# Float64 weights rounded to float32 by integer steps, with four raw blocks in flight and q, k loaded two head pairs ahead, in a routed attention and squared-ReLU kernel

## The chip, the cores and the metric

One core of one Trainium2 chip runs the whole kernel. The metric is the device time of one execution in microseconds (us). The kernel before takes 1234.09 us, the median of 3 runs (1233.55 to 1234.19).

## What is computed

The first part is attention in which a query sees only the keys of its own cluster: q and k rows are assigned to the nearest of 16 centroids per head. The second part is a feed-forward block on the result. Batch 4, 8 heads, 768 positions, head size 64; model size 512, inner size 2048.

```python
q_assign = np.argmax(np.einsum('bhsd,hcd->bhsc', q_n, c_n), axis=-1)   # q_n, c_n: unit length
k_assign = np.argmax(np.einsum('bhsd,hcd->bhsc', k_n, c_n), axis=-1)
scores = np.where(q_assign[..., :, None] == k_assign[..., None, :], scale * q @ k.T, -1e9)
attn = softmax(scores) @ v
x = attn.transpose(0, 2, 1, 3).reshape(B * S, H * D)
r = np.maximum(x @ w_in, 0.0)
return ((r * r) @ w_out).astype(np.float32)
```

q, k, v and the centroids are float32. w_in (512 x 2048) and w_out (2048 x 512) are float64, 16.8 MB together, and the kernel brings them to float32 itself.

## The kernel before

**Attention.** Heads are worked in 16 pairs (4 batches x 4 pairs). For a pair, `prep` turns q and k by matrix products into qkT (`turn`, three parts), makes the products with the centroids (`logits`) and the cluster numbers (`route`), and for the first batch one-hot masks (`turn_onehot`), for the others spread cluster numbers (`spread`). Then each half of the queries goes over 6 chunks of 128 keys: `scores` makes the products sc, ScalarE the exponentials ex (L337), and GpSimd adds them up in acc: five additions (L347, L351) for six exponentials. `times_v` multiplies by v, and `finish` divides by the sums: VectorE makes rb, ok and xT (L376 to L382).

**The unit.** The program is one list of 96 units; a unit is two key chunks of one pair and half, so two exponentials. The first 24 units are the first batch, all first halves before all second halves. `times_v` runs two units late.

**Feed-forward.** `ffn` is cut into steps, one matrix product each, that the main loop strews between the units as fill: ph (L395) with w_in, gT by ScalarE (L402) and squared by VectorE (L403), then po (L408) with w_out, osb and the store. The first fill stands behind unit 14. What fill is left after the last unit runs at the end.

**The weights.** A block is 128 rows of 512 weights; there are 16 of w_in and 16 of w_out. `load_weights` brings one raw block (512 KB, pool wstage, two buffers) as pairs of 32-bit words lo and hi. `round_weights` makes float32 of it: VectorE cuts out the exponent (w_power, L126), ScalarE shifts its origin (L129), VectorE bounds it (L130) and joins the sign (L134), VectorE cuts out the upper fraction (L139), ScalarE brings it and lo to floating point (L142, L143), GpSimd adds the two (L144) and multiplies by the power (L145). The temporary w_power has one buffer. The main loop asks for 4/3 blocks per unit in the first 12 units, then for two.

```python
for _ in range(2):
    load_weights(next(loaded))
...
rounding += 4 / 3 if u < 12 else 2
while rounding >= 1:
    rounding -= 1
    i = next(to_round, None)
    if i is not None:
        round_weights(i)
```

**What sets the order.** A scheduler at build time puts each engine's instructions in one fixed row, from the program's order and its own estimate of times. On the chip each engine takes its row in order. All loads and stores are issued by SyncE (SP), also in a fixed order; a load waits there until its buffer is free, and what is behind it waits too.

**The end.** The sums of `finish` are checked: good is reduced to one number (L512 ff.), a product every (L515) and a comparison make flag, and all engines read flag and jump over a general path that is not taken with these inputs.

Of the kernel before, what the change touches and what calls it, by code (L numbers as in the profile page):

```python
# [17 lines left out]
P = 128  # L18
UP = 2.0 ** 40
BIG = 2.0 ** 80  # L20


@with_exitstack
def kernel(
# [22 lines left out]
    NG = B * HP  # L47
    SCALE = float(D) ** -0.5
# [3 lines left out]
    loads = ctx.enter_context(tc.tile_pool(name="loads", bufs=3))  # L52
# [8 lines left out]
    xtp = ctx.enter_context(tc.tile_pool(name="xtp", bufs=3))  # L61
    gtp = ctx.enter_context(tc.tile_pool(name="gtp", bufs=FT))
    outp = ctx.enter_context(tc.tile_pool(name="outp", bufs=1))
    wstage = ctx.enter_context(tc.tile_pool(name="wstage", bufs=2))
    wtmp = ctx.enter_context(tc.tile_pool(name="wtmp", bufs=1))
# [52 lines left out]
    def round_weights(i):  # L118
        dst = weights[i][0]
        w = raw_w.pop(i)  # L120
        lo, hi = w[:, :, 0], w[:, :, 1]
        lo_f, hi_f = lo.bitcast(F32), hi.bitcast(F32)
        power = wtmp.tile([P, NW], U32, name="w_power")
        power_f = power.bitcast(F32)

        nc.vector.tensor_scalar(  # L126
            out=power, in0=hi, scalar1=0x7FF00000, scalar2=None, op0=ALU.bitwise_and
        )
        nc.scalar.activation(out=power_f, in_=power, func=ACT.Relu, bias=rebias, scale=1.0)  # L129
        nc.vector.tensor_scalar(  # L130
            out=power, in0=power_f, scalar1=float(255 << 20), scalar2=8.0,
            op0=ALU.min, op1=ALU.mult,
        )
        nc.vector.scalar_tensor_tensor(  # L134
            out=power, in0=hi, scalar=0x80000000, in1=power,
            op0=ALU.bitwise_and, op1=ALU.bitwise_or,
        )

        nc.vector.tensor_scalar(  # L139
            out=hi, in0=hi, scalar1=0x000FFFFF, scalar2=None, op0=ALU.bitwise_and  # L140
        )
        nc.scalar.activation(out=hi_f, in_=hi, func=ACT.Copy, bias=1.0, scale=2.0 ** -20)  # L142
        nc.scalar.mul(out=lo_f, in_=lo, mul=2.0 ** -52)  # L143
        nc.gpsimd.tensor_tensor(out=hi_f, in0=hi_f, in1=lo_f, op=ALU.add)  # L144
        nc.gpsimd.tensor_tensor(out=dst, in0=hi_f, in1=power_f, op=ALU.mult)  # L145


    cen = const.tile([P, D], F32, name="cen")
    nc.sync.dma_start(cen, centroids.rearrange("h c d -> (h c) d"))
    load_qk(0)  # L150
    load_v(0)
# [11 lines left out]
    rebias = const.tile([P, 1], F32, name="rebias")  # L163
    nc.vector.memset(rebias, -float((1023 - 127) << 20))
# [545 lines left out]
```

## Time and profile before

| | |
|---|---|
| median of 3 runs | 1234.09 us |
| the profiled execution's own time | 1233.24 us |
| its span in the trace | 1231.4 us |
| TensorE (PE) busy | 1135.8 us, 92% |
| VectorE (DVE) busy | 578.6 us, 47% |
| GpSimd (POOL) busy | 381.3 us, 31% |
| ScalarE (ACT) busy | 336.2 us, 27% |
| granted TensorE clock, mean | 0.953 |

PEld is TensorE's weight load, which runs beside its products. Times of instructions are from the profile of that one execution; "idle before, releaser" tells how long the engine stood before an instruction and what ended that. A float32 product is two instructions in the profile and one in the order rows below.

### The profile page before, as it was taken

How to read it: one execution, taken by the hardware profiler on the slowest of the kernel's cores; microseconds unless marked ns; L12 is line 12 of the kernel's file. 1: busy time of each engine (PE TensorE's matmuls, PEld its weight loads, DVE VectorE, ACT ScalarE, POOL GpSimd, SP SyncE). 2: the span in 40 equal slices, each digit the busy share in tenths (PEclk: the TensorE clock that was granted, in tenths of full speed). 3: DMA queues.
4: the chain of work that ended last, by engine and by line, in shares of the span. 5: the costliest groups of instructions: out<-in, count | busy, mean ns of one | idle time of the engine just before them, and what ended most of it. 6: DMA issues, size and time to landing. Idle time of an engine off the chain costs nothing.

```text
span 1231.4 us, 10628 instructions
## 1 busy us (share of the span) xinstructions
PE 1135.8 (92%) x4115; PEld 516.2 (42%) x4115; DVE 578.6 (47%) x795; ACT 336.2 (27%) x543; POOL 381.3 (31%) x233
## 2 busy tenths in 40 slices
PE   6677776689999999999999999999999999999997
PEld 3223232234444444444444444444444544554553
DVE  4466746441386865566445654266345653210110
ACT  4433343432233323232212231223212221110110
POOL 2655655442143433432232322233132332000000
PEclk7877798879999999999999999999999999999999
DMA  6332222211201101101001010201000000000000
GB/s 177 87 93 75 79 69 82 90 52 38 56 1 38 39 1 48 47 9 39 1 18 48 1 39 9 56 1 26 9 9 22 1 1 18 9 1 18 9 9 20
DMA packets 63881, 44.30 MB, mean 36 GB/s; under 512 B 51536, under 2 KB 56656, under 8 KB 63824
## 3 DMA queue, kind: packets, MB, share of 16 engines
q1 hardware_dynamic: 63824, 43.56, 12.4%
q8 instruction: 34, 0.56, 0.2%
q14 instruction: 23, 0.19, 0.0%
HBM read 37.26 MB, written 6.29 MB: 35 GB/s over the span
## 4 chain that ended last, share of the span: by engine, by line
PE 77%; POOL 8%; issue 8%; DVE 4%; ACT 2%; DMA 0%; SPq 0%; POOLq 0%; ACTq 0%
PE po L408 27%; PE ph L395 24%; PE sc L325 10%; PE av L357 9%; POOL acc L351 3%; POOL w_raw L144 2%; PE sm L372 2%; PE pt L227 2%; POOL w_out L145 1%; POOL w_in L145 1%; DVE w_power L126 1%; PE pb L303 1%; PE lg L243 1%; ACT ex L337 1%; DVE ids L269 0%
## 5 line engine op out<-in xcount | busy, mean ns | idle before, releaser
L395 PE MATMUL ph<-xT,w_in 128*128 128x384 f32 x1024 | 361.6, 502 | 27.4 <-ACT gT L402 26.3
L351 POOL TENSOR_TENSOR acc<-acc,ex 128x768 f32<-128x768 f32 x128 | 245.9, 1921 | 398.1 <-DVE ex L339 322.6
L408 PE MATMUL po<-w_out,gT 128*128 128x512 f32 x768 | 349.9, 602 | 0.0
L339 DVE SCALAR_TENSOR_TENSOR ex<-qid,ids,ex 128x384 f32<-128x384 bf16 x288 | 229.1, 847 | 157.9 <-ACT ex L337 157.7
L395 PEld LDWEIGHTS ph<-xT,w_in 128*128 128x128 f32 x1024 | 189.9, 193 | 186.9 <-issue 32.3
L408 PEld LDWEIGHTS po<-w_out,gT 128*128 128x128 f32 x768 | 140.5, 191 | 175.1 <-issue 170.6
L325 PE MATMUL sc<-qkT 64*128 64x384 f32 x768 | 195.0, 546 | 12.2 <-ACT ex L337 12.2
L337 ACT ACTIVATE ex<-sc 128x768 f32<-128x768 f32 x192 | 148.1, 806 | 197.0 <-PE sc L325 152.3
L403 DVE TENSOR_TENSOR gT<-gT 128x384 f32<-128x384 f32 x128 | 91.8, 721 | 177.7 <-ACT gT L402 177.4
L357 PE MATMUL av<-ex,v_raw 128*64 128x384 f32 x768 | 161.9, 521 | 0.0
L402 ACT ACTIVATE gT<-ph 128x384 f32<-128x384 f32 x128 | 62.5, 488 | 250.8 <-PE ph L395 250.8
L325 PEld LDWEIGHTS sc<-qkT 64*128 64x128 f32 x768 | 77.0, 197 | 105.1 <-issue 64.2
L376 DVE RECIPROCAL rb<-sm 128x384 f32<-128x384 f32 x32 | 81.7, 2554 | 80.6 <-PE sm L372 80.6
L347 POOL TENSOR_TENSOR acc<-ex 128x768 f32<-128x768 f32 x32 | 58.4, 1826 | 174.7 <-DVE ex L339 153.3
L357 PEld LDWEIGHTS av<-ex,v_raw 128*64 128x64 f32 x768 | 50.8, 141 | 93.3 <-issue 91.5
L126 DVE TENSOR_SCALAR w_power<-w_raw 128x512 uint32<-128x512 uint32 x32 | 32.6, 1020 | 78.0 <-POOL w_out L145 39.9
L415 ACT COPY osb<-po 128x512 f32<-128x512 f32 x24 | 14.0, 585 | 176.2 <-PE po L408 145.9
L144 POOL TENSOR_TENSOR w_raw<-w_raw 128x512 f32<-128x512 f32 x32 | 33.3, 1040 | 79.9 <-ACT w_raw L142 79.9
L129 ACT ACTIVATE w_power<-w_power,rebias 128x512 f32<-128x512 uint32 x32 | 23.1, 722 | 82.0 <-DVE w_power L126 82.0
L307 ACT CAST qid<-pb 128x384 bf16<-128x384 f32 x48 | 21.9, 480 | 40.2 <-PE pb L303 40.0
L142 ACT ACTIVATE w_raw<-w_raw 128x512 f32<-128x512 uint32 x32 | 21.4, 668 | 41.7 <-DVE w_raw L139 41.7
L372 PE MATMUL sm<-acc,ups 128*64 128x384 f32 x128 | 30.2, 536 | 2.7 <-ACT gT L402 2.7
(70 smaller groups left out, 423.2 us busy)
## 6 DMA issues: line engine op xcount, KB each, us to landing
w_raw<-in_moe_w_in_dram SPq DMA_DIRECT2D x16, 512.0 KB, 3.8
w_raw<-in_moe_w_out_dram SPq DMA_DIRECT2D x16, 512.0 KB, 3.5
v_raw<-in_v_dram SPq DMA_DIRECT2D x20, 384.0 KB, 3.2
q_raw<-in_q_dram SPq DMA_DIRECT2D x32, 192.0 KB, 3.6
k_raw<-in_k_dram SPq DMA_DIRECT2D x32, 192.0 KB, 3.2
out_dram<-osb SPq DMA_DIRECT2D x24, 256.0 KB, 2.0
cen<-in_centroids_dram SPq DMA_DIRECT2D x1, 32.0 KB, 1.7
```

What stands on the lines that cost most here:

```text
L144: nc.gpsimd.tensor_tensor(out=hi_f, in0=hi_f, in1=lo_f, op=ALU.add)
L325: nc.tensor.matmul(sc[:, e, 0:TB], lhsT=qkT[pair][rows, NCH + c], rhs=qkT[pair][rows, NB * h : NB * (h + 1)], start=True, stop=pair >= HP,)
L337: nc.scalar.activation(out=t, in_=sc[:, :, 0:TB], func=ACT.Exp, scale=SCALE)
L339: nc.vector.scalar_tensor_tensor(out=t[:, e], in0=qid[pair][1][:, h, e], scalar=ids[pair][:, c % NB, 2 + c // NB, e : e + 1], in1=t[:, e], ...
L347: nc.gpsimd.tensor_tensor(out=acc[pair, h], in0=ex[pair, h, 0], in1=t, op=ALU.add)
L351: nc.gpsimd.tensor_tensor(out=acc[pair, h], in0=acc[pair, h], in1=t, op=ALU.add)
L357: nc.tensor.matmul(av[pair, h][D * e : D * (e + 1)], lhsT=raw_v[pair][:, e, c], rhs=ex[pair, h, c][:, e], start=(c == 0), stop=(c == NCH - 1),
L376: nc.vector.reciprocal(out=rb, in_=sm)
L395: nc.tensor.matmul(ph, lhsT=w_in[:, kk, f * P : (f + 1) * P], rhs=xT[b, h][:, kk], start=(kk == 0), stop=(kk == KT - 1),)
L402: nc.scalar.activation(out=gT[f], in_=ph, func=ACT.Relu)
L403: nc.vector.tensor_tensor(out=gT[f], in0=gT[f], in1=gT[f], op=ALU.mult)
L408: nc.tensor.matmul(po, lhsT=gT[f][:, i * P : (i + 1) * P], rhs=w_out[:, f], start=(f == 0), stop=(f == FT - 1),)
```

## The change

`round_weights` becomes six steps. ScalarE takes the absolute value of hi, read as a float32, into the weight's place (L131) and makes of lo a small number beside 2.0 (L133). VectorE bounds the first (L136) and shifts it left by three bits (L140), and joins the sign of hi to the second (L143). GpSimd adds the two as 32-bit integers (L147). There is no temporary any more, and the constant rebias goes.

The raw blocks have four buffers instead of two. q and k are loaded two pairs ahead (pool loads with four buffers instead of three), v up to three units ahead, and the first v behind the first preparation. The loop asks for 3/2 blocks per unit in the first 12 units. To make room, the raw blocks and three start-up tiles lie in a part of the memory that is closed after the last block; the third xT buffer and two osb buffers (before: one) are opened there. best and ok share a buffer. The check of the sums is written ahead of the left-over fill.

```diff
+    AHEAD = 4
-    loads = ctx.enter_context(tc.tile_pool(name="loads", bufs=3))
+    loads = ctx.enter_context(tc.tile_pool(name="loads", bufs=4))
-    xtp = ctx.enter_context(tc.tile_pool(name="xtp", bufs=3))
+    xtp = ctx.enter_context(tc.tile_pool(name="xtp", bufs=2))
-    outp = ctx.enter_context(tc.tile_pool(name="outp", bufs=1))
-    wstage = ctx.enter_context(tc.tile_pool(name="wstage", bufs=2))
-    wtmp = ctx.enter_context(tc.tile_pool(name="wtmp", bufs=1))
+    early = ExitStack()
+    wstage = early.enter_context(tc.tile_pool(name="wstage", bufs=AHEAD, side="right"))
+    once_early = early.enter_context(tc.tile_pool(name="once_early", bufs=1, side="right"))
+    later = {}
...
     def round_weights(i):
-        dst = weights[i][0]
+        dst = weights[i][0].bitcast(U32)
         w = raw_w.pop(i)
         lo, hi = w[:, :, 0], w[:, :, 1]
-        nc.vector.tensor_scalar(
-            out=power, in0=hi, scalar1=0x7FF00000, scalar2=None, op0=ALU.bitwise_and
-        )
-        nc.scalar.activation(out=power_f, in_=power, func=ACT.Relu, bias=rebias, scale=1.0)
+        nc.scalar.activation(out=dst.bitcast(F32), in_=hi.bitcast(F32), func=ACT.Abs)
+        nc.scalar.activation(
+            out=lo.bitcast(F32), in_=lo, func=ACT.Copy, bias=2.0, scale=2.0 ** -51
+        )
         nc.vector.tensor_scalar(
-            out=power, in0=power_f, scalar1=float(255 << 20), scalar2=8.0,
-            op0=ALU.min, op1=ALU.mult,
+            out=dst.bitcast(F32), in0=dst.bitcast(F32), scalar1=2.0 ** -15, scalar2=HIGHEST,
+            op0=ALU.max, op1=ALU.min,
+        )
+        nc.vector.tensor_scalar(
+            out=dst, in0=dst, scalar1=3, scalar2=None, op0=ALU.logical_shift_left
         )
         nc.vector.scalar_tensor_tensor(
-            out=power, in0=hi, scalar=0x80000000, in1=power,
-            op0=ALU.bitwise_and, op1=ALU.bitwise_or,
-        )
-        nc.vector.tensor_scalar(
-            out=hi, in0=hi, scalar1=0x000FFFFF, scalar2=None, op0=ALU.bitwise_and
-        )
-        nc.scalar.activation(out=hi_f, in_=hi, func=ACT.Copy, bias=1.0, scale=2.0 ** -20)
-        nc.scalar.mul(out=lo_f, in_=lo, mul=2.0 ** -52)
-        nc.gpsimd.tensor_tensor(out=hi_f, in0=hi_f, in1=lo_f, op=ALU.add)
-        nc.gpsimd.tensor_tensor(out=dst, in0=hi_f, in1=power_f, op=ALU.mult)
+            out=lo, in0=hi, scalar=0x80000000, in1=lo, op0=ALU.bitwise_and, op1=ALU.bitwise_or
+        )
+        dst, lo = dst.bitcast(I32), lo.bitcast(I32)
+        nc.gpsimd.tensor_tensor(out=dst, in0=dst, in1=lo, op=ALU.add)
...
     load_qk(0)
-    load_v(0)
+    load_qk(1)
...
             raw.pop(pair)
-            load_qk(pair + 1)
+            load_qk(pair + 2)
...
-            xT[b, h] = xtp.tile([P, KT, TB], F32, name="xT")
+            pool = xtp if (2 * b + h) % 3 < 2 else later["xT"]
+            xT[b, h] = pool.tile([P, KT, TB], F32, name="xT")
...
-    for _ in range(2):
+    for _ in range(AHEAD):
         load_weights(next(loaded))
...
-            if c == 0 and pair not in raw_v:
-                load_v(pair)
+            if c == 0 and u + 3 < len(units) and units[u + 3][0] not in raw_v:
+                load_v(units[u + 3][0])
...
-        rounding += 4 / 3 if u < 12 else 2
+        rounding += 3 / 2 if u < 12 else 2
...
+            elif not later:
+                early.close()
+                for name, bufs in (("xT", 1), ("out", 2)):
+                    later[name] = ctx.enter_context(
+                        tc.tile_pool(name=name + "_late", bufs=bufs, side="right",
+                                     reuse_waits="tile")
+                    )
```

How the instructions move is seen on two engines.

GpSimd, the first blocks, before (w_raw with a number is one raw block, w_in the rounded weights, acc the sums of exponentials):

```order
L144 TENSOR_TENSOR w_raw_263<-w_raw_263 128x512
L145 TENSOR_TENSOR w_in_109<-w_raw_263,w_power_367 128x512
L351 TENSOR_TENSOR acc_251<-acc_251,ex_351 128x768
L351 TENSOR_TENSOR acc_251<-acc_251,ex_359 128x768
L144 TENSOR_TENSOR w_raw_316<-w_raw_316 128x512
L145 TENSOR_TENSOR w_in_109<-w_raw_316,w_power_409 128x512
L347 TENSOR_TENSOR acc_403<-ex_394,ex_401 128x768
```

and with the change:

```order
L351 TENSOR_TENSOR acc_258<-acc_258,ex_366 128x768
L147 TENSOR_TENSOR w_in_106<-w_in_106,w_raw_266 128x512
L147 TENSOR_TENSOR w_in_106<-w_in_106,w_raw_315 128x512
L147 TENSOR_TENSOR w_in_106<-w_in_106,w_raw_323 128x512
L347 TENSOR_TENSOR acc_406<-ex_397,ex_404 128x768
L147 TENSOR_TENSOR w_in_106<-w_in_106,w_raw_380 128x512
```

Ahead of the first addition of the second pair (L347 into acc_403, acc_406) GpSimd has four blocks done before and seven with the change. The last of the 32 blocks comes after 36 additions of acc before, and after 25 now.

ScalarE where the feed-forward's first results gT come, before (ex_978 is the 31st exponential):

```order
L337 ACTIVATE ex_978<-sc_973 128x768
L143 ACTIVATE w_raw_865<-w_raw_865 128x512
L142 ACTIVATE w_raw_824<-w_raw_824 128x512
L402 ACTIVATE gT_1015<-ph_1010 128x384
L129 ACTIVATE w_power_901<-w_power_901,rebias_134 128x512
L402 ACTIVATE gT_1023<-ph_1018 128x384
L142 ACTIVATE w_raw_865<-w_raw_865 128x512
```

and with the change (ex_933 is the 31st, w_raw_1069 the 32nd block):

```order
L337 ACTIVATE ex_925<-sc_920 128x768
L131 ACTIVATE w_out_107<-w_raw_1061 128x512
L133 ACTIVATE w_raw_1061<-w_raw_1061 128x512
L337 ACTIVATE ex_933<-sc_928 128x768
L131 ACTIVATE w_out_107<-w_raw_1069 128x512
L133 ACTIVATE w_raw_1069<-w_raw_1069 128x512
L403 ACTIVATE gT_962<-ph_957 128x384
L403 ACTIVATE gT_970<-ph_965 128x384
```

Before, 17 blocks are through GpSimd when the 31st exponential is made, and the others stand between the exponentials and gT of the next eight units. Now all 32 stand ahead of the first gT. On TensorE the products keep their places from unit to unit: the feed-forward's steps stand at the same units in both.

## Rows read from the trace of the kernel before

**Rows 1.** The page, the span in 40 slices of 30.8 us.
```profile
PE   6677776689999999999999999999999999999997
PEclk7877798879999999999999999999999999999999
```

**Rows 2.** Stretches: length, then each engine's busy us (instructions), granted clock, DMA share, GB/s.
```profile
core 0: us, PE busy (x) PEld busy (x) DVE busy (x) ACT busy (x) POOL busy (x), PEclk, DMA share, GB/s
0.00:13.00 13.00, 4.84 (x19) 2.98 (x19) 4.53 (x23) 2.60 (x4) 2.21 (x9) 1.00 0.81 213
13.00:166.00 153.00, 111.09 (x474) 46.41 (x474) 88.82 (x115) 66.56 (x102) 86.20 (x59) 0.77 0.32 89
166.00:309.70 143.70, 111.18 (x369) 49.89 (x371) 59.75 (x90) 50.69 (x84) 63.88 (x45) 0.86 0.21 66
309.70:1223.50 913.80, 908.49 (x3254) 416.85 (x3251) 425.35 (x567) 215.76 (x355) 229.00 (x120) 1.00 0.07 20
```

**Rows 3.** ScalarE's timeline at the 31st and 32nd exponential, and at the 49th.
```profile
165.37 1.49 ACT L337 ACTIVATE ex<-sc 128x768 f32<-128x768 f32 x2
...
309.67 1.51 ACT L337 ACTIVATE ex<-sc 128x768 f32<-128x768 f32 x2 [3.93 <-PE sc L325]
```

**Rows 4.** Waits from 13 to 275 us: who for whom, us, times, longest.
```profile
ACT w_power L129 <- DVE w_power L126: 82.0, 29, 4.8
POOL w_raw L144 <- ACT w_raw L142: 79.9, 24, 13.9
DVE w_power L126 <- POOL w_out L145: 39.9, 15, 5.5
```

**Rows 5.** Instructions on w_raw and w_power: ns min/median/max, first and last start.
```profile
L143 ACT ACTIVATE w_raw<-w_raw x32: 657/672/723, 12.5 to 267.6; 128x512 f32<-128x512 uint32 x32
L126 DVE TENSOR_SCALAR w_power<-w_raw x32: 411/427/2014, 12.5 to 268.7; 128x512 uint32<-128x512 uint32 x32
L134 DVE SCALAR_TENSOR_TENSOR w_power<-w_raw,w_power x32: 627/692/2174, 14.7 to 271.2; 128x512 uint32<-128x512 uint32 x32
L144 POOL TENSOR_TENSOR w_raw<-w_raw x32: 1036/1039/1048, 16.7 to 273.1; 128x512 f32<-128x512 f32 x32
L145 POOL TENSOR_TENSOR w_in<-w_raw,w_power x16: 1288/1292/1492, 17.8 to 156.9; 128x512 f32<-128x512 f32 x16
...
L130 DVE TENSOR_SCALAR w_power<-w_power x32: 409/427/1566, 14.3 to 269.9; 128x512 uint32<-128x512 f32 x32
```

**Rows 6.** Timeline of all engines, 34 to 43 us (GpSimd and VectorE).
```profile
36.48 1.80 POOL L351 TENSOR_TENSOR acc<-acc,ex 128x768 f32<-128x768 f32 x1
36.55 2.01 DVE L126 TENSOR_SCALAR w_power<-w_raw 128x512 uint32<-128x512 uint32 x1 [2.88 <-POOL w_in L145]
38.48 0.55 DVE L260 TENSOR_TENSOR best<-lt,mx 128x384 bf16<-128x384 f32 x1
39.06 0.56 DVE L264 TENSOR_TENSOR best<-best,order 128x384 bf16<-128x384 bf16 x1
40.16 1.81 POOL L351 TENSOR_TENSOR acc<-acc,ex 128x768 f32<-128x768 f32 x1 [1.88 <-ACT ex L337]
40.34 2.17 DVE L134 SCALAR_TENSOR_TENSOR w_power<-w_raw,w_power 128x512 uint32<-128x512 uint32 x1
```

**Rows 7.** TensorE's groups from 310 to 1200 us: busy us, mean ns, idle before.
```profile
L395 PE MATMUL ph<-xT,w_in 128*128 128x384 f32 x896 | 308.9, 494 | 0.0
L408 PE MATMUL po<-w_out,gT 128*128 128x512 f32 x654 | 296.8, 599 | 0.0
L325 PE MATMUL sc<-qkT 64*128 64x384 f32 x570 | 132.0, 514 | 0.0
L357 PE MATMUL av<-ex,v_raw 128*64 128x384 f32 x592 | 117.1, 499 | 0.0
L372 PE MATMUL sm<-acc,ups 128*64 128x384 f32 x100 | 21.7, 511 | 0.0
```

**Rows 8.** Timeline of all engines at the end.
```profile
1223.63 0.58 ACT L415 COPY osb<-po 128x512 f32<-128x512 f32 x1 [13.15 <-PE po L408]
1223.70 0.15 DVE L516 TENSOR_SCALAR flag<-every 1x1 int32<-1x1 f32 x1 [40.24 <-PE every L515]
1224.24 0.33 SPq L416 DMA_DIRECT2D out_dram<-osb  x1
```

More of the change, by code (lines that the diff above doesn't have):

```diff
@@ L20 @@
 BIG = 2.0 ** 80
+HIGHEST = 1.875 * 2.0 ** 16
 @with_exitstack
@@ L118, in round_weights @@
     def round_weights(i):
[L119 removed]
+        dst = weights[i][0].bitcast(U32)
         w = raw_w.pop(i)
         lo, hi = w[:, :, 0], w[:, :, 1]
[L122 to L124 removed]
+        nc.scalar.activation(out=dst.bitcast(F32), in_=hi.bitcast(F32), func=ACT.Abs)
+        nc.scalar.activation(
+            out=lo.bitcast(F32), in_=lo, func=ACT.Copy, bias=2.0, scale=2.0 ** -51
+        )
         nc.vector.tensor_scalar(
[L127 removed]
+            out=dst.bitcast(F32), in0=dst.bitcast(F32), scalar1=2.0 ** -15, scalar2=HIGHEST,
+            op0=ALU.max, op1=ALU.min,
         )
[L129 removed]
         nc.vector.tensor_scalar(
[L131 to L132 removed]
+            out=dst, in0=dst, scalar1=3, scalar2=None, op0=ALU.logical_shift_left
         )
         nc.vector.scalar_tensor_tensor(
[L135 to L148 removed]
+            out=lo, in0=hi, scalar=0x80000000, in1=lo, op0=ALU.bitwise_and, op1=ALU.bitwise_or
+        )
+        dst, lo = dst.bitcast(I32), lo.bitcast(I32)
+        nc.gpsimd.tensor_tensor(out=dst, in0=dst, in1=lo, op=ALU.add)
+    cen = once_early.tile([P, D], F32, name="cen")
     nc.sync.dma_start(cen, centroids.rearrange("h c d -> (h c) d"))
     load_qk(0)
[L151 removed]
+    load_qk(1)
     ident = const.tile([P, P], F32, name="ident")
@@ L162 @@
     nc.vector.tensor_copy(out=order, in_=order_i)
-    rebias = const.tile([P, 1], F32, name="rebias")
-    nc.vector.memset(rebias, -float((1023 - 127) << 20))
     good = const.tile([P, 2 * NG], F32, name="good")
-    oh = const.tile([P, NB, 4, 2, D], BF16, name="oh")
+    oh = once_early.tile([P, NB, 4, 2, D], BF16, name="oh")
     nc.gpsimd.memset(oh, 0.0)
@@ L175, in centroids_norm @@
     def centroids_norm():
-        sq = const.tile([P, D], F32, name="cen_sq")
+        sq = once_early.tile([P, D], F32, name="cen_sq")
         ss = const.tile([P, 1], F32, name="cen_ss")
@@ L258, in route @@
         nc.vector.reduce_max(out=mx, in_=lt, axis=AX.X)
-        best = once.tile([P, n, C], BF16, name="best")
+        best = once.tile([P, n, C], BF16, name="best", tag="b")
         nc.vector.tensor_tensor(
@@ L376, in finish @@
         nc.vector.reciprocal(out=rb, in_=sm)
-        ok = once.tile([P, TB], BF16, name="ok")
+        ok = once.tile([P, TB], BF16, name="ok", tag="b")
         nc.vector.scalar_tensor_tensor(
@@ L413, in ffn @@
                     yield
-            osb = outp.tile([P, DM], F32, name="osb")
+            osb = later["out"].tile([P, DM], F32, name="osb")
             nc.scalar.copy(out=osb, in_=po)
@@ L454 @@
         item()
+    load_v(0)
     ahead = []
@@ L505 @@
                 left_units[0] = NCH * HP // 2 if b == 0 and h == 0 else NCH * HP
-    for g in fill:
-        for _ in g:
-            pass
     flag = const.tile([P, 1], I32, name="flag")
@@ L518 @@
     )
+    for g in fill:
+        for _ in g:
+            pass
     ctx.close()
```

## The prediction

> **What bounds the kernel now.** I read the slices first. TensorE is full from the tenth slice on and at six to seven tenths before, and there its granted clock is lowered [rows 1]. The stretches say the same in us: from 309.7 to 1223.5 us TensorE is busy 908.49 of 913.80 us at clock 1.00, so nothing on another engine can shorten that part, and whatever comes earlier in front of it shifts the end one for one [rows 2]. The change acts ahead of it. The 49th exponential, the first one of the second batch, starts at 309.67 us, the 31st at 165.37 [rows 3]; I use both as marks, because with the change the last block stands right behind the 31st.
>
> Why is TensorE not full there? The waits show a ring [rows 4]: VectorE's first step of a block (L126) waits for GpSimd's last step of the block before (39.9 us for w_out alone, since w_power has one buffer), ScalarE's L129 waits for L126 (82.0 us), GpSimd's L144 for ScalarE (79.9 us). One block costs its whole chain.
>
> Under the ring lies a second bound. An L126 takes 0.43 us in the median and 2.01 at most [rows 5]. In the timeline the 2.01 us one starts at 36.55, just behind an acc that GpSimd began at 36.48 and ended at 38.28, and it ends 0.28 us behind that; an L134 of 2.17 us stands in the same way behind the acc at 40.16. Meanwhile L260, which reads PSUM, keeps its 0.55 us [rows 6]. So VectorE's steps that read only on-chip memory through two paths (L126, L130, L134, L139, L264 and their like) and GpSimd's additions take turns; I call their common time the shared port and add it up.
>
> Port time up to the 31st exponential, before: 17 blocks x (1.04 + 1.29 on GpSimd, 3 x 0.43 + 0.69 on VectorE = 4.31) = 73.3 us; 25 acc x 1.80 [rows 6] = 45.0; 13 other VectorE steps (best, oh, ok, gT) x 0.56 = 7.3. Together 125.6 us of the 153 us from the first block (L126 at 12.5 [rows 5]) to 166: 82%. So even with the ring the port is more than four fifths full.
>
> **The change, part by part.**
>
> *Rounding.* Port time per block goes from 4.31 us to two one-input steps at 0.43 (L136, L140, priced as L126 and L130), one joining step at 0.69 (as L134) and one GpSimd step: 1.55 us plus the integer add. No row shows an integer add of this size on GpSimd. Below it stands L144 at 1.04 us, above it L145 at 1.29, whose operands (one packed, one with gaps, packed result) are those of the new step [rows 5]. I take 1.29 and keep 1.04; upward the rows give no end, and a rival takes that. The Trainium skill ("GPSIMD Engine Reference", Performance versus the Vector engine) gives about 2.6 cycles per element for a two-input step; 512 elements at 1.2 GHz would be 1.11 us, an estimate, and the result would come out some 6.5 us lower. This case's L145 is above that, and the measured row decides.
>
> ScalarE loses L129 and keeps two steps like L143 (0.67 us [rows 5]); with 66.56 us busy in 153 [rows 2] it bounds nothing, so that is worth nothing by itself.
>
> *Four blocks in flight, no w_power.* The ring is gone: VectorE may be several blocks ahead of GpSimd. What is left is the port, and the fixed orders in which a step can stand behind one that waits.
>
> *Where the blocks stand.* All 32 now stand ahead of the 31st exponential, 17 before. So the first 15.5 units carry more rounding than they did. Port time to that mark: 32 x (1.55 + 1.29) = 90.9, acc 45.0, others 7.3: 143.2 us, more than the 125.6 of before. That is why I don't expect the saved 1.47 us per block to show one for one.
>
> *Loads.* With two pairs of q, k and v ahead of the first block, about 2.5 MB must land first; at the 213 GB/s of the first 13 us [rows 2] that is 11.8 us, as late as before. The next three blocks stand behind a third pair, 1.3 MB or 6 us more. Half of that gap I count as lost, so the port's work begins at 15 us. The 32 blocks of 512 KB and q, k, v of six pairs, 25 MB or less in some 165 us, need 150 GB/s, which is below those 213: hidden. A block's load waits on SP for GpSimd's add four blocks earlier, and q, k, v loads wait behind it; being two pairs ahead they have six units of cover. Without that cover each would cost a turn about its landing time, some 4 us.
>
> *After the last block.* From there to the 49th exponential TensorE has, by count of the order and price [rows 7], 68 sc x 0.232 + 72 av x 0.198 + 108 ph x 0.345 + 60 po x 0.454 + 12 sm x 0.217 = 97 us at full clock. Masks and one pair's preparation come to that; TensorE's whole busy time there was 111 at clock 0.86 [rows 2], so it lies between 97 and 111, and I take 106. ScalarE and VectorE have no blocks in between any more, so TensorE sets the pace, as it does behind 309.7 us.
>
> *The end.* flag is done at 1223.85, before osb is copied (1224.21) and stored [rows 8]; taking it off the end is worth nothing. The second osb buffer and the shared best/ok buffer (both VectorE) cost and bring nothing where TensorE is full.
>
> **The sum.** How full can the port be? 0.82 with the ring; without it more, but in fixed order and with TensorE at lowered clock not 1. I take 0.88, keep 0.80 and 0.97. The 31st exponential and last block: 15 + 143.2 / 0.88 = 178 us, later than the 166 of before. The 49th: 178 + 106 = 284 instead of 309.7. That is 26 us less, 1207 us against the profiled execution's 1233.24; the median of the runs is 0.85 higher, so **1208 us**. With 0.97 and an add of 1.04 us: 15 + 139 + 104 = 258, a gain of 52, 1182 us. With 0.80: 15 + 179 + 109 = 303, a gain of 7, 1227 us.
>
> **The rivals.**
>
> *Slower: the integer add is long.* 26 us are used up when the add takes 26 x 0.88 / 32 = 0.7 us more than 1.29, that is from 2.0 us on. At twice L145, 2.6 us, it costs 48 us, and the time is about 1256 us. For it: no row of such an add. Against it: L144 and L145 differ by only a quarter for other work on the same sizes. 10%.
>
> *No gain: crowding.* With all blocks ahead of the 31st exponential, ScalarE's first step of a block waits for its load with exponentials behind it. If the port is then only 0.74 full, 15 + 194 + 106 = 315 us, and the time is 1239; at 0.76 it is 1233 or so. For it: TensorE has 111 us of work there at clock 0.77 [rows 2], three quarters of the stretch, and its gaps lower the clock. Against it: before, the port reached 0.82 with a worse chain. 7%, half of it within 0.2%.
>
> *More gain: the new steps don't take turns.* Then TensorE is the bound from the start: its 111 us of busy time at clock 0.77 begin with the first exponential's chain near 20 us, so the mark comes at 131 to 145, the 49th at 237 to 251, and the time is 1160 to 1176 us. The Trainium skill ("GPSIMD Engine Reference", Specifications) says that GpSimd shares its memory interfaces with VectorE and names contention with steps in a two-port mode or with two inputs there; all three new VectorE steps are such, so by that rule this rival falls. The trace agrees with its 2.01 against 0.43 us [rows 5]. 7%.
>
> *It doesn't do what it says:* the four buffers fill no faster, because SP's row holds the loads. A chain of load, ScalarE, VectorE and GpSimd per block of 8 us or so would, for 32 blocks, push the mark to 270 us and the time to 1290. The order has loads four ahead and nothing that waits longer between; 2%.
>
> **How the numbers follow.** The forecast, a port-bound first stretch, has 74% and by itself 1182 to 1227. Below 1178 I leave out most of the optimistic rival, above 1236 most of the long add. Two runs can be told apart from about 0.2%, 2.5 us, on. Faster 0.82: the forecast but for a small part at its upper end, the optimistic rival, and an add of between 1.3 and 2 us. Same 0.05. Slower 0.13: the long add, half the crowding, the serial case and what I overlooked.
>
> **What would show it.** Right: GpSimd's L147 near 1.29 us and VectorE's L136 and L140 at 0.43 or, behind an addition, near 2; the last L147 near 178 us; the 31st exponential not earlier than before, and the 49th near 284; TensorE full from about 180 us on, at clock 1.00. Wrong: an L147 above 2 us; long waits of ScalarE's L131 for loads; an L136 running beside an acc at 0.43 us; or a last block before 150 us.

## The result, and the profile after

| | before | after |
|---|---|---|
| median of the runs (4 of each, on one chip) | 1233.82 us | 1181.81 us (1179.31 to 1182.77) |
| span of the profiled execution | 1231.4 us | 1179.1 us |
| 31st exponential starts | 165.4 | 153.5 |
| last block leaves GpSimd | 275.5 | 155.2 |
| 49th exponential starts | 309.7 | 253.6 |
| last osb is copied | 1223.6 | 1173.2 |

The changed kernel takes 0.9576 of the time of before [0.9559, 0.9593], 52 us less, where 26 were forecast. The sign, the place and the turns of VectorE and GpSimd were as predicted; the gain was twice the forecast.

The page's slices of the changed kernel, here of 29.5 us each:

```profile
PE   5666699999999999999999999999999999899997
PEclk8887799999999999999999999999999999999999
```

TensorE is full from the sixth slice on; before it was from the tenth [rows 1]. One slice near the end shows an 8 that before did not have; it comes back below.

The stretches of the changed kernel, with the columns of [rows 2], cut at the same marks (the 31st exponential, the 49th, the last copy of osb), and one window of 20 us around that 8:

```profile
13.00:153.50 140.50, 93.34 (x445) 40.88 (x446) 129.79 (x141) 70.03 (x111) 92.88 (x56) 0.79 0.51 153
153.50:253.60 100.10, 99.29 (x395) 46.47 (x393) 25.40 (x34) 25.47 (x40) 29.07 (x16) 1.00 0.09 23
253.60:1173.20 919.60, 910.34 (x3255) 417.83 (x3251) 425.54 (x568) 215.77 (x355) 229.00 (x120) 1.00 0.07 19
1000.00:1020.00 20.00, 16.09 (x48) 8.65 (x47) 6.06 (x10) 2.54 (x5) 0.00 (x0) 0.91 0.04 13
```

The first row holds all the rounding: VectorE is recorded busy for 129.79 of 140.50 us, against 88.82 of 153.00 before. It does more there, 96 rounding steps (three on each of 32 blocks) against 68 (four on each of 17), and a busy record includes the time in which a step waits for its turn (rows of 0.41 and of 2.0 us for one step, below), so the engine's busy share says little here. In the second row TensorE is busy 99.29 of 100.10 us at clock 1.00; before, the way between the same two marks took 143.70 us at clock 0.86 [rows 2]. The third row is nearly 6 us longer than before.

The two marks in ScalarE's timeline of the changed kernel, to be read beside [rows 3]:

```profile
153.49 1.62 ACT L337 ACTIVATE ex<-sc 128x768 f32<-128x768 f32 x2 [1.81 <-PE sc L332]
...
253.65 1.51 ACT L337 ACTIVATE ex<-sc 128x768 f32<-128x768 f32 x2 [3.93 <-PE sc L325]
```

The rounding steps of the changed kernel (instructions on w_raw and w_in: ns least, median, most, first and last start), to be read beside [rows 5]:

```profile
L133 ACT ACTIVATE w_raw<-w_raw x32: 645/668/695, 15.0 to 144.5; 128x512 f32<-128x512 uint32 x32
L143 DVE SCALAR_TENSOR_TENSOR w_raw<-w_raw x32: 677/1776/2318, 16.7 to 152.9; 128x512 uint32<-128x512 uint32 x32
...
L147 POOL TENSOR_TENSOR w_out<-w_out,w_raw x16: 1276/1400/1539, 98.9 to 153.6; 128x512 int32<-128x512 int32 x16
...
L136 DVE TENSOR_SCALAR w_in<-w_in x16: 405/414/2026, 15.1 to 83.3; 128x512 f32<-128x512 f32 x16
...
L140 DVE TENSOR_SCALAR w_in<-w_in x16: 410/1211/2025, 15.9 to 83.7; 128x512 uint32<-128x512 uint32 x16
```

The integer add takes 1.40 us in the median (1.29 was taken); 24 of the 32 start while an L136 is under way, and these are the ones of 1.39 to 1.49. In the kernel with the arithmetic alone, below, where the blocks stand less densely, the median is 1.29: the add itself costs what was taken. The first L136 starts at 15.1 us (15 was taken). The joining step L143, 0.68 us when nothing is beside it, has a median of 1.78: most of the 32 stand behind a GpSimd instruction that is under way.

The waits of the changed kernel from 13 to 155 us, as in [rows 4]:

```profile
POOL w_in L147 <- DVE w_raw L143: 26.8, 9, 14.7
PE po L284 <- DVE oh L271: 25.0, 4, 8.1
...
ACT w_out L131 <- DMA w_raw<-in_moe_w_out_dram: 22.6, 12, 4.5
```

The ring of [rows 4], with its 82.0, 79.9 and 39.9 us, is gone. What TensorE itself waits for longest is now oh, VectorE's masks, which stand in VectorE's row among the rounding steps (25.0 us in four waits).

### The profile page after: what moved, and what is told of

It is laid out like the page before. It is cut to its first block, busy times and chain, and to the rows that moved or that the text cites. A ratio compares the mean times of both kernels' runs of the same rounds, so it can differ in the third digit from the quotient of the medians.

```text
span 1179.1 us, 10496 instructions
## 1 busy us (share of the span) xinstructions
PE 1109.5 (94%) x4115; PEld 508.6 (43%) x4115; DVE 584.8 (50%) x762; ACT 315.0 (27%) x511; POOL 353.2 (30%) x201
## 4 chain that ended last, share of the span: by engine, by line
PE 86%; DVE 7%; issue 3%; POOL 2%; DMA 1%; ACT 1%; SPq 1%; POOLq 0%; DVEq 0%; ACTq 0%
PE ph L396 29%; PE po L409 29%; PE sc L325 11%; PE av L357 10%; PE sm L373 2%; DVE w_raw L143 2%; PE pt L227 2%; PE pb L303 1%; PE lg L243 1%; POOL w_out L147 1%; DVE w_in L136 1%; POOL acc L351 1%; DVE ids L269 1%; DVE best L264 1%; DMA w_raw<-in_moe_w_out_dram 1%
## 5 line engine op out<-in xcount | busy, mean ns | idle before, releaser
L396 PE MATMUL ph<-xT,w_in 128*128 128x384 f32 x1024 | 356.9, 499 | 6.7 <-DVE xT L383 6.7
L325 PE MATMUL sc<-qkT 64*128 64x384 f32 x768 | 183.4, 523 | 12.6 <-ACT ex L337 12.6
L357 PE MATMUL av<-ex,v_raw 128*64 128x384 f32 x768 | 158.5, 513 | 0.0
L325 PEld LDWEIGHTS sc<-qkT 64*128 64x128 f32 x768 | 73.0, 189 | 99.6 <-issue 58.4
L347 POOL TENSOR_TENSOR acc<-ex 128x768 f32<-128x768 f32 x32 | 59.5, 1860 | 177.2 <-DVE ex L339 153.2
L143 DVE SCALAR_TENSOR_TENSOR w_raw<-w_raw 128x512 uint32<-128x512 uint32 x32 | 49.1, 1535 | 1.9 <-ACT w_raw L133 1.9
L232 ACT COPY qkT<-pt 128x512 f32<-128x512 f32 x32 | 18.7, 586 | 57.1 <-PE pt L227 57.0
L147 POOL TENSOR_TENSOR w_in<-w_in,w_raw 128x512 int32<-128x512 int32 x16 | 22.7, 1417 | 32.5 <-DVE w_raw L143 26.8
L230 DVE COPY qkT<-pt 128x512 f32<-128x512 f32 x16 | 11.0, 689 | 40.3 <-PE pt L227 40.3
L284 PE MATMUL po<-ident_b,oh 128*128 128x128 bf16 x48 | 5.9, 298 | 25.0 <-DVE oh L271 25.0
```

Of the source, the lines that this page charges most:

```text
L143: nc.vector.scalar_tensor_tensor(out=lo, in0=hi, scalar=0x80000000, in1=lo, op0=ALU.bitwise_and, op1=ALU.bitwise_or)
L325: nc.tensor.matmul(sc[:, e, 0:TB], lhsT=qkT[pair][rows, NCH + c], rhs=qkT[pair][rows, NB * h : NB * (h + 1)], start=True, stop=pair >= HP,)
L347: nc.gpsimd.tensor_tensor(out=acc[pair, h], in0=ex[pair, h, 0], in1=t, op=ALU.add)
L357: nc.tensor.matmul(av[pair, h][D * e : D * (e + 1)], lhsT=raw_v[pair][:, e, c], rhs=ex[pair, h, c][:, e], start=(c == 0), stop=(c == NCH - 1),
L396: nc.tensor.matmul(ph, lhsT=w_in[:, kk, f * P : (f + 1) * P], rhs=xT[b, h][:, kk], start=(kk == 0), stop=(kk == KT - 1),)
```

## The experiments

Two theories were to be told apart. By the port theory the way to the 49th exponential is set by the time in which GpSimd and VectorE take turns at the port; by the ring theory it is set by the chain of one block, which four buffers and no w_power cut open. A third question was what the blocks' place (all ahead of the 31st exponential) and the check's place each do. All kernels here compute the whole of the reference.

**The arithmetic alone.** The kernel before with the new `round_weights` and nothing else: two raw blocks, q and k one pair ahead, 4/3 blocks per unit, the check where it was.

```diff
-    wtmp = ctx.enter_context(tc.tile_pool(name="wtmp", bufs=1))
...
     def round_weights(i):
-        dst = weights[i][0]
+        dst = weights[i][0].bitcast(U32)
...
```

> The kernel before with the new rounding steps alone: two raw blocks, 4/3 blocks per unit, loads and check as before. Port theory (VectorE's and GpSimd's steps take turns, and the saved 1.5 to 1.9 us of port time per block is the gain; dropping w_power opens the ring by itself, two raw blocks being enough for most of it): last block at 180 to 210 us, 1185 to 1200 us. Rival (the blocks in flight bring the gain; with two, load, ScalarE, VectorE and GpSimd stay in a ring of 8 us per two blocks): last block beyond 230 us, 1210 us or more.

Measured: 1176.52 us, ratio 0.9538 [0.9522, 0.9554]. That is faster than either theory expected. The new arithmetic alone brings all of the gain; the rest of the change adds nothing to it, and the whole of it takes some 5 us more (1181.81), for which the check of the sums, below, accounts. The edit takes w_power away too, and with it VectorE's wait for GpSimd's last step of the block before, so by itself it doesn't part the steps from the ring; the next kernel and the one with one raw block do. The blocks here are spread over a longer stretch (instructions on w_raw and on w_out; VectorE's line is L139 and GpSimd's L143 in this kernel):

```profile
L139 DVE SCALAR_TENSOR_TENSOR w_raw<-w_raw x32: 628/684/2298, 14.2 to 177.2; 128x512 uint32<-128x512 uint32 x32
...
L143 POOL TENSOR_TENSOR w_out<-w_out,w_raw x16: 1277/1289/1731, 105.5 to 177.9; 128x512 int32<-128x512 int32 x16
```

The last block ends at 179.4 us instead of 155.2, yet the 49th exponential starts at 253.4, as in the changed kernel (253.6). The joining step stays at its 0.68 us in the median: spread out, the blocks meet fewer of GpSimd's instructions. So it is not the place of the blocks that counts.

**The new order with the old arithmetic.** The changed kernel with the nine old steps, w_power in two buffers and three raw blocks in flight.

```diff
-    AHEAD = 4
+    AHEAD = 3
...
+    wtmp = early.enter_context(tc.tile_pool(name="wtmp", bufs=2, side="right"))
...
```

> The change with the old nine-step rounding, w_power in two buffers and three raw blocks: the ring is open, the steps and their port time are as before. Port theory (the port time per block counts): about 4 us per block by start-to-start times, 188 us to the last block behind 30 additions; last block at 210 us or later, the 49th exponential at 280 us or later, 1200 to 1215 us. Ring theory (the one w_power buffer was what held the blocks): 49th exponential at 250 to 262 us, 1177 to 1190 us.

Measured: 1221.24 us, ratio 0.991 [0.9894, 0.9925]; last block at 220.1 us, 49th exponential at 291.4. The port theory's marks held and its time was too low. An open ring with the old steps is worth 18 us at the 49th exponential and 12 in time (this kernel has the check of the sums in its new place, which costs some 5 us, below); the new steps with two raw blocks are worth 56 in both. The stretches of this kernel behind the 31st exponential show what the longer rounding costs TensorE:

```profile
172.00:220.00 48.00, 32.32 (x101) 15.35 (x101) 38.75 (x45) 22.38 (x38) 32.72 (x23) 0.82 0.26 85
220.00:291.00 71.00, 70.19 (x278) 31.75 (x278) 16.22 (x22) 17.21 (x27) 18.43 (x11) 1.00 0.10 26
```

While blocks are left, TensorE is busy 32.32 of 48.00 us at clock 0.82; once they are through, 70.19 of 71.00 at 1.00.

**Two raw blocks in the changed kernel** (`AHEAD = 2`, everything else kept).

```diff
-    AHEAD = 4
+    AHEAD = 2
```

> The change with two raw blocks in flight instead of four. Port theory: the port stays the bound, loads are hidden but for single waits, last block at 155 to 175 us, 1182 to 1195 us. Rival (four in flight bring most of it): last block beyond 200 us, 1205 us or more.

Measured: 1183.26 us (1175.99 to 1185.68), ratio 0.9606 [0.9588, 0.9625]. Its profiled execution, at the lower end, has the last block at 180.1 us, 5 later than expected, and the 49th exponential at 248.8. Between two and four buffers no gain can be told.

**One raw block** (`AHEAD = 1`): now the ring is as tight as it can be made, with the new steps in it.

```diff
-    AHEAD = 4
+    AHEAD = 1
```

> The change with one raw block in flight: the new steps with little port time, but a ring of load (3.6 us), ScalarE, VectorE and GpSimd of about 8 us per block, as long as the old ring. Ring theory: last block at 260 to 285 us, 49th exponential at 295 to 315 us, 1220 to 1240 us, about the time before. Port theory (the ring never was the bound): last block before 230 us, 49th exponential at 260 to 280 us, 1185 to 1205 us.

Measured: 1202.6 us, ratio 0.9748 [0.9731, 0.9764]. Its instructions on w_out and its waits from 13 to 272 us:

```profile
L147 POOL TENSOR_TENSOR w_out<-w_out,w_raw x16: 1275/1407/1601, 153.5 to 270.9; 128x512 int32<-128x512 int32 x16
```

```profile
ACT w_out L131 <- DMA w_raw<-in_moe_w_out_dram: 62.5, 15, 6.1
...
DVE w_out L136 <- ACT w_out L131: 67.7, 16, 8.4
```

The ring is there: from the first to the last of these 16 blocks it is 117.4 us, 7.8 us each, with VectorE waiting 67.7 us for ScalarE and ScalarE 62.5 us for loads. The last block ends at 272.5 us, 3 us ahead of before (275.5). And still the 49th exponential starts at 266.6, 43 us sooner than before. Each theory got one mark: the blocks end where the ring theory put them, the time is what the port theory gave. A late last block by itself costs much less than the old steps did: this kernel is 21 us slower than the changed one, 13 of them ahead of the 49th exponential and 8.6 behind it (928.2 us to the last osb instead of 919.6), where the last block still stands.

**One more VectorE step.** The bounding step is written twice, which leaves the value as it is and adds 32 one-input steps.

```diff
+        nc.vector.tensor_scalar(
+            out=dst.bitcast(F32), in0=dst.bitcast(F32), scalar1=2.0 ** -15, scalar2=HIGHEST,
+            op0=ALU.max, op1=ALU.min,
+        )
```

> The change with VectorE's bounding step written twice per block (the second changes nothing): 32 x 0.33 to 0.43 = 11 to 14 us more port time. Port theory: last block at 163 to 170 us, 49th exponential 8 to 14 us later than with the change, 1189 to 1196 us. Rival (the way to the 49th exponential is set by TensorE's own work at its lowered clock): 49th exponential within 3 us of the change's 253.6, 1180 to 1185 us.

Measured: 1186.97 us, ratio 0.9626 [0.9613, 0.964]. The last block ends at 165.2 us, 10.0 later, which is 0.31 us per step added. The row gives 0.41 for such a step when it is alone:

```profile
L140 DVE TENSOR_SCALAR w_out<-w_out x16: 395/414/2033, 96.8 to 161.1; 128x512 f32<-128x512 f32 x16
```

The 49th exponential came only 4.5 us later and the time rose by 5, between the theory's 1189 to 1196 and the rival's 1180 to 1185. The order explains most of the difference. Here are the 31st exponential and GpSimd's last two adds of this kernel (L341 and L151 here):

```profile
159.09 1.50 ACT L341 ACTIVATE ex<-sc 128x768 f32<-128x768 f32 x2
160.79 1.54 POOL L151 TENSOR_TENSOR w_out<-w_out,w_raw 128x512 int32<-128x512 int32 x1 [1.64 <-DVE w_out L144]
163.63 1.53 POOL L151 TENSOR_TENSOR w_out<-w_out,w_raw 128x512 int32<-128x512 int32 x1 [1.30 <-DVE w_out L144]
```

Two adds start behind the 31st exponential where the changed kernel has one, so one block less stands ahead of it. The mark comes 5.6 us later (159.1 instead of 153.5), and with the 2.8 us of that one block the delay of the port's work ahead of it is 8.4. From the mark to the 49th exponential it is 99.0 us, 1.2 less than in the changed kernel. So the added steps delay the blocks by what their port time is, and the block that moved behind the mark cost nothing there.

**Additions of acc moved from GpSimd to VectorE.** For the pairs of the first batch the sums of h = 0 (20 additions) are made on VectorE.

```diff
+    def on_vector(pair, h, c):
+        return pair < HP and h == 0
...
+            adder = nc.vector if on_vector(pair, h, c) else nc.gpsimd
...
```

> The change, with the 20 additions of acc of the first 12 units on VectorE instead of GpSimd. Port theory (the shared time of both engines bounds the first stretch; an addition takes 1.80 us of it on GpSimd and near 0.85 on VectorE): 20 x 0.95 = 19 us less port time, last block at 130 to 140 us, 1162 to 1172 us. Rival (VectorE by itself bounds the stretch, 112 us busy of 123): 17 us more work for it, last block at 165 us or later, 1190 us or more.

Measured: 1171.47 us, ratio 0.95 [0.947, 0.953]; the 49th exponential comes 10 us earlier (243.6). From 75 to 136 us, first the changed kernel, then this one:

```profile
75.00:136.00 61.00, 42.76 (x208) 17.03 (x209) 59.83 (x61) 29.62 (x46) 45.49 (x28) 0.81 0.51 155
```

```profile
75.00:136.00 61.00, 46.55 (x210) 18.16 (x207) 57.10 (x72) 30.86 (x48) 29.13 (x18) 0.82 0.48 153
```

GpSimd is busy 16 us less, and VectorE does 72 instructions instead of 61 in slightly less busy time. Ahead of the 31st exponential TensorE waits 13.5 us for oh instead of 25.0, and 5.1 instead of 12.6 for exponentials. One miss: the last block was expected between 130 and 140 us and ended at 154.5, as in the changed kernel. A part of that is not this edit's, as the kernel with both edits shows below.

**The check of the sums, put back** behind the left-over fill, where it was before.

```diff
+    for g in fill:
+        for _ in g:
+            pass
     flag = const.tile([P, 1], I32, name="flag")
...
```

> The change, but with the check of the sums behind the left-over fill, as before. Theory (the check in front of the fill makes TensorE wait 3.9 us for VectorE's sum of good and lowers its clock after that, 5.6 us from the 49th exponential to the last osb, while the end behind the last osb gets 1.9 us shorter): no wait of every any more, the last osb 5.6 us sooner after the 49th exponential, the end 1.9 us longer, 1178 us. Rival, the prediction's own term (the check is worth nothing either way): as the change, 1181 to 1182 us.

Measured: 1176.52 us (1176.18 to 1178.31), ratio 0.955 [0.9537, 0.9563]. What TensorE waits for behind the 49th exponential, first in the changed kernel, then in this one (both lists are whole):

```profile
PE pb L303 <- DVE ids_b L279: 5.3, 9, 0.8
PE every L520 <- DVE fine L518: 3.9, 1, 3.9
```

```profile
PE pb L303 <- DVE ids_b L279: 5.3, 9, 0.8
```

The wait is gone, and from the 49th exponential to the last osb it is 914.0 us instead of 919.6. Behind the last osb it is 7.2 us instead of 5.9, 1.4 longer, where 1.9 were expected. VectorE's timeline of the changed kernel at that place shows why TensorE had to wait there:

```profile
1002.26 2.56 DVE L377 RECIPROCAL rb<-sm 128x384 f32<-128x384 f32 x1 [23.30 <-PE sm L373]
1004.85 0.56 DVE L379 SCALAR_TENSOR_TENSOR ok<-rb 128x384 bf16<-128x384 f32 x1
...
1005.33 0.55 DVE L383 SCALAR_TENSOR_TENSOR xT<-av,rb 128x384 f32<-128x384 f32 x1
1005.80 0.17 DVE L518 TENSOR_REDUCE fine<-good 128x1 f32<-128x32 f32 x1
```

The check reads the last sums, so its product stands behind four VectorE steps that begin only when the sums are there. Left-over products that could have filled these 3.9 us stand behind the check in TensorE's row. The granted clock of the window from 1000 to 1020 us is 0.91; the missing 0.09 are 1.8 us of its 20, an estimate, and with the 3.9 they make up the 5.6 us.

**The check inside the left-over fill**: 16 fill steps first, then the check, then the rest.

```diff
+    left[0] = 10 ** 6
+    fill_steps(16)
     flag = const.tile([P, 1], I32, name="flag")
...
```

> The change with the sum of good and then 16 steps of the left-over fill ahead of the product every: TensorE has work while VectorE makes the sum, and the check is off the end. Theory: no wait of every, last osb as with the check behind (914 us after the 49th exponential), the end behind the last osb as with the change (5.9 us); 1174 to 1176 us, faster than the check behind the fill by about 1.5 us. Rival (the flag's place doesn't matter for the end): 1176 to 1178 us.

Measured: 1176.64 us, ratio 0.9538 [0.9525, 0.9551]. The wait for fine is gone, 914.6 us from the 49th exponential to the last osb, and the end behind it is as short as in the changed kernel (5.8 us). In the trace it takes both halves; in the medians it can't be told from the check put back, and 1176.64 lies in the rival's range.

**Both together**: the check inside the fill and the 20 additions on VectorE.

> The change with the 20 additions of acc of the first 12 units on VectorE and the product every inside the left-over fill. If the two gains add (10 us at the 49th exponential from the first, 5 us at the end from the second): 49th exponential at 243 to 246 us, 1164 to 1168 us. If they don't, because the first one's run varies by several us between executions: 1168 to 1174 us.

Measured: **1157.27 us**, ratio 0.9401 [0.9374, 0.9428], 24.5 us below the changed kernel and faster than expected. The 49th exponential starts at 235.0 us. Its first stretch:

```profile
13.00:75.00 62.00, 47.78 (x263) 21.59 (x262) 55.07 (x80) 37.76 (x60) 20.37 (x14) 0.89 0.66 189
```

With the additions alone this stretch had clock 0.75 and 222 instructions of TensorE; here it has 0.89 and 263. Yet the two programs have the same instructions in the same order on TensorE, VectorE, ScalarE and GpSimd up to the 49th exponential, which the one reaches at 243.6 us and the other at 235.0. The 8.6 us arise between 25 and 100 us, most of them where TensorE is busy all the time, at one level of its clock or at the other. From 63 to 73 us, first with the additions alone, then with both edits:

```profile
63.00:73.00 10.00, 10.00 (x27) 3.40 (x26) 6.37 (x9) 2.99 (x7) 2.67 (x2) 0.50 0.17 54
```

```profile
63.00:73.00 10.00, 10.00 (x60) 4.08 (x56) 9.86 (x16) 6.80 (x11) 4.10 (x3) 1.00 0.48 121
```

At clock 0.50, its lower level of 1.2 GHz, TensorE has 27 instructions in this window, and at 1.00 it has 60. So these 8.6 us come from neither edit; two executions of the same rows lie so far apart (on two chips, on which the kernel before takes 1232.6 and 1233.9 us). The times of both kernels scatter by about that much (1165.99 to 1175.51 us with the additions alone, 1156.23 to 1167.85 here), and the sum of the two gains, 10.3 and 5.2 us, gives 1166.3, which lies among those of this kernel.

**Both, with two raw blocks** (`AHEAD = 2` on top).

> The same with two raw blocks instead of four. Port theory, VectorE now being the one that is full in the first stretch: fewer blocks stand ahead of the 31st exponential, the rest goes beside TensorE's fill; 31st exponential before 140 us, 49th at 238 to 246 us, 1160 to 1168 us. Rival (with two blocks the loads come late once the port has room): 49th exponential beyond 250 us, 1172 us or more.

Measured: 1158.68 us (1157.83 to 1161.43), ratio 0.9394 [0.9382, 0.9406]: the same. Its last block ends at 170.2 us instead of 145.8. So the additional gain does not hang on four buffers either, and the kernel with two does as well.

**Both, with only the additions of even c** on VectorE (8 of the 20).

```diff
+        return pair < HP and h == 0 and c % 2 == 0
```

> As with both, but only 8 of the 20 additions on VectorE (those of the third and fifth chunk). Port theory with turns: an addition costs VectorE 0.85 us of its own and saves it a wait of up to 1.8 us; with 8 the gain is 8/20 of the 10 us: 49th exponential near 250 us, 1170 to 1173 us. If VectorE's own work was the limit with all 20: at or below 243 us, 1160 to 1166 us.

Measured: 1169.14 us, ratio 0.9477 [0.9465, 0.9489]. It lies 7.5 us below the check inside the fill without any addition moved, and all 20 lie 19.4 below it, which would be 0.94 and 0.97 us for each addition. But without the edit of the check the 20 brought 10.3, or 0.52 each, with the same rows up to the 49th exponential. So eight additions gain and 20 gain more; in what proportion, these runs don't show. The 49th exponential comes at 245.6 us, which neither expectation had (near 250, or at most 243).

**q and k one pair ahead**, four raw blocks kept.

```diff
-    loads = ctx.enter_context(tc.tile_pool(name="loads", bufs=4))
+    loads = ctx.enter_context(tc.tile_pool(name="loads", bufs=3))
...
-    load_qk(1)
...
-            load_qk(pair + 2)
+            load_qk(pair + 1)
```

> The change with q and k one pair ahead and three buffers for them, as before. Theory (loads are hidden either way, the DMA moves 162 GB/s in the first stretch and had moved 213 at the start): within 3 us of the change, 1179 to 1185 us. Rival (being two pairs ahead is what lets the preparation of a pair start in time): 49th exponential 10 us or more later, 1190 us or more.

Measured: 1189.94 us, ratio 0.9646 [0.9634, 0.9658]: 8 us slower than the change, between theory and rival. Its longest wait of TensorE from 13 to 160 us, and its stretch from 13 us to the 31st exponential:

```profile
PE po L283 <- DVE oh L270: 24.8, 4, 10.8
```

```profile
13.00:160.30 147.30, 100.56 (x450) 41.51 (x452) 129.14 (x141) 69.40 (x111) 92.61 (x57) 0.76 0.47 140
```

TensorE waits as long for oh as in the changed kernel (25.0), and among its waits none is for a load of q or k. So the 8 us don't come from q and k landing late. In the trace 6.8 of them stand ahead of the 31st exponential, and they are not idle time: TensorE is busy 100.56 us instead of 93.34 for nearly the same products (450 and 445 records), at clock 0.76 instead of 0.79. The blocks stand still further ahead here (the last one ends at 150.1, while the 31st exponential comes at 160.3). With two raw blocks one pair ahead loses nothing (the arithmetic alone, 1176.52), so it may be that the second pair pays for what four blocks in flight cost. Why the clock is lower here was not separated.

## Why the prediction came out too small

**What bounds the kernel: right.** What is won ahead of the 49th exponential reaches the end one for one, but for the check. 309.67 - 253.65 = 56.0 us are won ahead of it, 5.6 lost behind it, 1.9 won behind the last osb (5.9 instead of 7.8): 52.3, which is the difference of the spans, 1231.4 - 1179.1.

**The mechanism, taking turns: right.** The timeline of the changed kernel at its densest, first VectorE, then GpSimd:

```profile
119.34 0.68 DVE L143 SCALAR_TENSOR_TENSOR w_raw<-w_raw 128x512 uint32<-128x512 uint32 x1
119.95 0.41 DVE L136 TENSOR_SCALAR w_out<-w_out 128x512 f32<-128x512 f32 x1
120.28 1.77 DVE L143 SCALAR_TENSOR_TENSOR w_raw<-w_raw 128x512 uint32<-128x512 uint32 x1
121.97 0.41 DVE L140 TENSOR_SCALAR w_out<-w_out 128x512 uint32<-128x512 uint32 x1
122.31 0.41 DVE L136 TENSOR_SCALAR w_out<-w_out 128x512 f32<-128x512 f32 x1
122.64 1.78 DVE L143 SCALAR_TENSOR_TENSOR w_raw<-w_raw 128x512 uint32<-128x512 uint32 x1
...
120.10 1.40 POOL L147 TENSOR_TENSOR w_out<-w_out,w_raw 128x512 int32<-128x512 int32 x1 [1.91 <-DVE w_raw L143]
122.47 1.41 POOL L147 TENSOR_TENSOR w_out<-w_out,w_raw 128x512 int32<-128x512 int32 x1 [0.96 <-DVE w_out L140]
124.84 1.40 POOL L147 TENSOR_TENSOR w_out<-w_out,w_raw 128x512 int32<-128x512 int32 x1 [0.97 <-DVE w_out L140]
```

The two L143 that start beside an add end 0.54 and 0.55 us behind the add's end; the one at 119.34, which has no add beside it, takes 0.68. The rival without turns falls. The Trainium skill ("GPSIMD Engine Reference", Specifications) names this contention; the trace agrees and adds the size, a step of 0.68 us lasting 1.78.

One of the rows that the prediction read for the turns doesn't bear on them: the L260 of 38.48 us keeps its 0.55 us, but the acc in front of it ended at 38.28, so nothing stood beside it. Another row of the kernel before bears the reading out. L258 reads lt from PSUM and keeps its 0.56 us beside two additions of acc that go on to 34.15:

```profile
30.42 3.73 POOL L351 TENSOR_TENSOR acc<-acc,ex 128x768 f32<-128x768 f32 x2 [1.62 <-ACT ex L337]
...
33.11 0.56 DVE L258 TENSOR_REDUCE mx<-lt 128x24 f32<-128x384 f32 x1 [2.70 <-PE lt L254]
```

**The failed step is the price of the port: "two one-input steps at 0.43, one joining step at 0.69".** The timeline of VectorE and GpSimd above has one block every 2.37 us (120.10, 122.47, 124.84), where the prediction reckoned 1.55 + 1.29 = 2.84. A row's duration runs on past the moment at which the next step of the same engine may start: L140 starts at 121.97 and L136 at 122.31, 0.34 us later and not 0.41; the L143 at 119.34 is followed at 119.95, after 0.61 us and not 0.68. Added durations count that overlap twice: by the distances from start to start the three steps take 0.61 + 0.34 + 0.33 = 1.28 us instead of 1.55, which is 0.27 of the 0.47 us. The other 0.20 lie where the engines change turns: the add of 122.47 starts while the L136 of 122.31 is under way. The distances of VectorE's steps were to be had from the trace of before; a dense row of whole blocks was not in it. With 2.37 the port's work is 32 x 2.37 + 25 x 1.80 + 13 x 0.47 (0.56 less the same 0.09) = 127 us instead of 143.2; at the chosen 0.88 that is (143.2 - 127) / 0.88 = 18 of the 24.5 us by which the 31st exponential came before the predicted 178. The other 6 are the port's fill (from 15.1 to 155.2 us it is 127 / 140 = 0.91) and the 1.7 us by which the last block ends behind the mark. The one added step agrees, at 0.31 us. So the 31st exponential came earlier than before (153.5 instead of 165.4), where the prediction had it no earlier.

**After the last block: a term 6 us too large.** 106 was taken between the counted 97 and the 111 of before; it measured 100.1, with TensorE full. The count by groups was the better guide.

**"Taking it off the end is worth nothing": wrong.** Behind the last osb 1.9 us are won, of which the check put back takes 1.4 again, and its new place costs 5.6 ahead of it: 3.7 us lost in all. The prediction took the check's old place for free, since osb was copied after flag, and did not ask what the check waits for at the new one.

Together: 25.7 + 24.5 + 5.8 - 3.7 = 52.3 us, the difference of the spans. That the time came out at the 1182 us of the prediction's favourable sum is chance: that sum had the port 0.97 full and an add of 1.04 us, and measured were 0.91 and no add below 1.28.

**Where the blocks stand, and four in flight.** The prediction's sum hangs the 49th exponential on the last block, 106 us behind it. In the changed kernel all blocks do stand ahead of the 31st exponential, and the distance is near that. But it is no rule of this kernel: with the arithmetic alone the last block ends at 179.4 us and the 49th exponential comes 74 us later, at the same time as in the changed kernel; with one raw block it comes ahead of the last block's end, and only 13 us later than in the changed kernel. The port's time per block counts, the block's place much less. Opening the ring is worth 18 us at the 49th exponential with the old steps, and with the new ones four buffers instead of two are worth nothing that can be measured.

**The rivals.** The long add falls: 1.28 to 1.59 us, waits included, far from the 2.0 from which it would have decided. The Trainium skill's figure ("GPSIMD Engine Reference", Performance versus the Vector engine), by which the estimate was 1.11, is below every one of the 32 adds, so that going by the row was right. Crowding falls: ScalarE waits 26.7 us for loads (22.6 for those of w_out, in pieces of at most 4.5, and 4.1 for those of w_in), and the port is 0.91 full. The serial case falls as well: 32 blocks take 140 us, 4.4 each and not 8.

**What is not shown.** By what way the saved port time reaches TensorE in all is argued from its longest wait alone, that for oh: 25.0 us in the changed kernel, 29.1 with the added step, 13.5 with the additions moved. Open are the 0.20 us per block where the engines change turns, what made the granted clock differ between two executions of the same rows (0.50 and 1.00 from 63 to 73 us), and why it is lower with q and k one pair ahead.

## What to carry to other kernels

Where two engines take turns at one resource, add up its time by the distance from one start to the next in a dense stretch, not by the durations of single rows: here the difference was 18 of the 26 us that were missed. A buffer that opens a chain is worth little when the resource under the chain is full, and fewer or cheaper steps on it are worth nearly everything, the ones of neighbouring work included (20 additions moved to the other engine brought 10 us in one kernel and 19 in another). A step that is taken off the end has to be asked what it waits for at its new place: put it behind some work that doesn't depend on it. And two kernels with the same rows up to a mark can reach it 8.6 us apart, at another granted clock: a difference of that size between two traces says nothing yet about an edit.

## What was not expected of the hardware

A VectorE step that shares its turn with GpSimd is recorded as busy while it waits: 0.41 us became 2.0 and 0.68 became 1.78 or more, so that VectorE's 129.79 busy us in 140.50 are for a large part waiting. GpSimd's adds show the same in small: 1.28 us at least, 1.40 where they start while an L136 is under way. An addition of acc, 1.80 us at least on GpSimd, takes 1.10 us in the mean on VectorE, its waits included:

```profile
L356 POOL TENSOR_TENSOR acc<-acc,ex 128x768 f32<-128x768 f32 x16 | 30.6, 1911 | 35.3 <-ACT ex L340 34.8
...
L356 DVE TENSOR_TENSOR acc<-acc,ex 128x768 f32<-128x768 f32 x16 | 17.7, 1104 | 0.9 <-ACT ex L340 0.9
```

(groups of instructions from 13 to 240 us in the kernel with the 20 additions moved and the check as in the change: busy us, mean ns, idle before).
